# Attention with a routed expert layer: a slot's tokens as whole rows through DRAM, in place of quarter rows gathered straight

## The chip, the cores and the metric

The kernel runs on one core of a Trainium2 chip. The metric is the device time of one execution in microseconds (us). Before the change it is 1119.16 us, the median of 3 runs between 1118.36 and 1120.58. The core has a matmul engine (TensorE, PE in the rows), three engines for elementwise work (VectorE or DVE, ScalarE or ACT, GpSimd or POOL), a queue engine that does nothing but start transfers (SyncE or SP), an on-chip memory of 128 partitions and 16 DMA engines that all queues share.

## The reference

```
q, k, v: (8, 12, 448, 64)                       # batch, heads, positions, head size
attn = softmax(rmsnorm(q, g_q) @ rmsnorm(k, g_k).T / 8) @ v
x = attn as 3584 rows of 768                    # one row for each token, the 12 heads side by side
logits = x @ w_gate + modality_bias[modality_id]
e = argmax(logits);  p = softmax(logits)[e]     # one of 8 experts for each token
out[token] = p * (relu(x[token] @ w1[e]) @ w2[e])     # w1: 768 x 1024, w2: 1024 x 768
```

All is float32. The kernel splits an operand into a rounded high part and the rest, and makes a product out of three matmuls.

## The kernel before

**Attention.** The 96 heads are worked off as 48 units of two heads, each in 7 steps, so that step `n` belongs to unit `n // 7`. Every engine runs its instructions in the order in which the program issues them; one loop over `n` (from L1278) issues for each step what a table (`PLAN`) has due: the score matmuls `st` (L953), the matmuls with the values `av` (L992), the row sums `sums` (L1009, tiles `sm`), whose addends GpSimd forms in `csum` (L968, tiles `r2w`, `at_hhw`, `at_w2hb`), the transposes. SyncE starts the loads of q, k and v, small moves between partitions (L868), the row maxima of a unit (`mt`, L940, the move at L948) and the stores of finished rows of x to the DRAM tensor `x_d` (L1072). The second matmul of each `st` step reads the row that L948 moves, so that unit 47 can't begin its scores before its move has landed.

**Routing.** After each batch the logits give the expert of each token; `route_put` (L1152) scatters (token, weight) pairs of 8 bytes into lists in DRAM, `l_d`, four scatters a batch. GpSimd issues them, and each waits until the one before has landed. Those of batches 6 and 7 are issued in slots 0 and 1.

**Experts.** The tokens of an expert are cut into blocks of 256, called slots; 14 of them (`NSTAT`) are always run, with the same program. A slot is 144 matmuls of the first product (`mm1_half`, tiles `ph`) and 96 of the second (`mm2_step`, tiles `py`). In the loop over slots (L1444) 8 half blocks of the first product and 16 steps `b_` of the second are issued in turn, and other work is hung between them at `beat` numbers: the half blocks are beats 0 to 7, step `b_` is beat `b_ + 8`. The work of one slot for later ones is: weight loads (`wload`, GpSimd), the splits `split1` and `split2` (ACT and VectorE, tiles `w1w`, `w2ha`, `w2lw`), the second half `hlw` of the hidden values (VectorE), the results' scatter to `out` (GpSimd, from the tile `yw`), and the tokens.

**A slot's tokens.** The list is fetched from `l_d` (`get`, L337, tile `ltn`), eight entries to a partition, and the same in each of four groups of 32 partitions. `fin` (L348) makes from it the indices of quarter rows (`xi`) and an ordered copy (`ltq`). `xload` (L495) issues 8 gathers on GpSimd, each with one quarter row of 768 bytes for each of 128 partitions: group g of 32 partitions holds quarter g of all 256 tokens. `xturn` (L513) then transposes on VectorE 32 by 32, in three parts, from `xrw` into a piece of `yw`; two copies (tiles `xw`) follow, and those are the operands of the first product. `yw` also holds the results on their way out, so a part of `xturn` waits for the scatter of the slot before it. `xrw` has two halves: slot s uses half s % 2. Slot 0 is gathered during unit 45 (L1374), slot 1 in the section after the attention loop (L1421), slot 2 in slot 0, slot 3 at the start of slot 2 (L1457), and every later slot two slots ahead at the steps `XLB` (L1501).

Of the kernel before, what the change touches and what calls it, by code (L numbers as in the profile page):

```python
# [9 lines left out]
F32 = mybir.dt.float32  # L10
# [56 lines left out]
def kernel(  # L67
# [24 lines left out]
    l_d = dp.tile([NE * NT, 2], F32, name="l_d")  # L92

# [53 lines left out]
    def gate_consts():  # L147
        GP.tensor_copy(out=m1, in_=modr.rearrange("p b (c w) -> p (b c) w", w=2)[:, :, 0])
        GP.tensor_scalar(out=m0, in0=m1, scalar1=-1.0, scalar2=1.0, op0=ALU.mult, op1=ALU.add)
        shp = [CP, B * NCH, NE]  # L150
        GP.tensor_tensor(out=ball, in0=m0.unsqueeze(2).to_broadcast(shp),
                        in1=bia[:, 0:1, :].to_broadcast(shp), op=ALU.mult)
        GP.tensor_tensor(out=btmp, in0=m1.unsqueeze(2).to_broadcast(shp),
                        in1=bia[:, 1:2, :].to_broadcast(shp), op=ALU.mult)
        GP.tensor_tensor(out=ball, in0=ball, in1=btmp, op=ALU.add)
        for tf, ti in iotas:
            GP.tensor_copy(out=tf, in_=ti)
        for g in range(1, 4):
            GP.memset(i_q[32 * g : 32 * g + 32], float(g))
        V.scalar_tensor_tensor(out=i_j, in0=i_q, scalar=-32.0, in1=i_pt[:, 0:1], op0=ALU.mult, op1=ALU.add)  # L160
        V.scalar_tensor_tensor(out=i_pn[:, 0:1], in0=i_j, scalar=8.0, in1=i_q, op0=ALU.mult, op1=ALU.add)
        V.tensor_scalar(out=i_pn[:, 1:2], in0=i_pn[:, 0:1], scalar1=4.0, scalar2=None, op0=ALU.add)
        V.tensor_copy(out=i_qi, in_=i_q.to_broadcast([128, 8]))
        GP.tensor_scalar(out=ie8, in0=i_e[:, 0:NE], scalar1=float(NE), scalar2=None, op0=ALU.add)
        GP.tensor_scalar(out=i_ebase, in0=i_e[:, 0:NE], scalar1=float(NT), scalar2=None, op0=ALU.mult)
# [21 lines left out]
    ltn = cp.tile([128, NSTAT, 8, 2], F32, name="ltn")  # L187
    lto = cp.tile([128, NS1 + NS2 - NSTAT, 2, 2], F32, name="lto")
    ltq = cp.tile([128, NSTAT, 2, 2], F32, name="ltq")
    xi = cp.tile([128, NSTAT, 8], I32, name="xi")  # L190
    i_q = cp.tile([128, 1], F32, name="i_q")
    V.memset(i_q, 0.0)
    i_j = cp.tile([128, 1], F32, name="i_j")
    i_pn = cp.tile([128, 2], F32, name="i_pn")
    i_qi = cp.tile([128, 8], I32, name="i_qi")

    def entry(s, t):
        return ltq[:, s, t] if s < NSTAT else lto[:, s - NSTAT, t]
# [24 lines left out]
    def tables(nm, ns, cnt, nb, taken, e_prev, half_blocks=None):  # L223
# [69 lines left out]
        V.tensor_scalar(out=eb[:, 0:nn], in0=js[:, 0:nn], scalar1=float(NE * NT - TB), scalar2=0.125,  # L293
                        op0=ALU.min, op1=ALU.mult)
        V.tensor_scalar(out=lr, in0=eb[:, 0:nn], scalar1=i_j[:, 0:1], scalar2=None, op0=ALU.add)
        ix = tl("ix", s2)
        for a, b_, pt in ((0, nn, i_pn), (nn, ns, i_pt)):
            if a < b_:
                sp = [128, b_ - a, 2]
                V.tensor_tensor(out=ix[:, a:b_], in0=js[:, a:b_].unsqueeze(2).to_broadcast(sp),  # L300
                                in1=pt.unsqueeze(1).to_broadcast(sp), op=ALU.add)
# [28 lines left out]
    def lists(nm, s0, ns, tb):  # L330
# [4 lines left out]
        rows = l_d.rearrange("(r w) c -> r (w c)", w=8)  # L335
# [12 lines left out]
        def fin(a, n):  # L348
            r, d = slice(a, a + n), slice(s0 + a, s0 + a + n)
            if s0 + a < NSTAT:  # L350
                V.scalar_tensor_tensor(out=xi[:, d], in0=ltn[:, d, :, 0].bitcast(I32), scalar=4.0,
                                       in1=i_qi.unsqueeze(1).to_broadcast([128, n, 8]),
                                       op0=ALU.mult, op1=ALU.add)
                for g in range(4):
                    p = slice(32 * g, 32 * g + 32)
                    V.tensor_copy(out=ltq[p, d], in_=ltn[p, d].rearrange("p s (t w) c -> p s t w c", t=2)[:, :, :, g])
                tid = ltq[:, d, :, 0].bitcast(I32)
            else:
                o = slice(s0 + a - NSTAT, s0 + a + n - NSTAT)
                tid = lto[:, o, :, 0].bitcast(I32)  # L360
# [131 lines left out]
    def xv(s):  # L492
        return view(xrw, 2 * DM * (s % 2), 128, 8, DM // 4)

    def xload(s, gs_=range(8)):  # L495
        tb, i = tb_of(s)
        if s < NSTAT:
            x = xv(s)
            src = x_d[:NT1] if s < NS1 else x_d[:]
            for g in gs_:  # L500
                G.indirect_dma_start(out=x[:, g], out_offset=None,
                                     in_=src.rearrange("t (g d) -> (t g) d", g=4),
                                     in_offset=IOFF(ap=xi[:, s, g : g + 1], axis=0))
            return x
# [246 lines left out]
    if True:  # L751
# [487 lines left out]
        XLB = (1, 2, 3, 5, 6, 7, 9, 10)  # L1239
# [38 lines left out]
        for n in range(P["start"], NJ * NU):  # L1278
# [95 lines left out]
            if n == NJ * (NU - 3) + 4:  # L1374
                xload(0)
# [45 lines left out]
        xload(1)  # L1421
# [22 lines left out]
        for s in range(NSTAT):  # L1444

            beat = {}
            if s + 1 < NSTAT:
                for g, (m, c) in enumerate(zip(XTB, XCB) if s else zip(XTB0, XCB0)):
                    at(beat, m, lambda m=m, c=c, g=g: at(beat, c, xturn(s + 1, g)))
            if s > 0:  # L1450
# [5 lines left out]
                if s == 2:  # L1456
                    at(beat, 1, lambda: xload(3))  # L1457
# [23 lines left out]
            for b_ in range(16):  # L1481
# [19 lines left out]
                if s != 1 and s + 2 < NSTAT and b_ in XLB:  # L1501
                    xload(s + 2, (XLB.index(b_),))
# [68 lines left out]
```

## Time and profile before

| | |
|---|---|
| median of 3 runs | 1119.16 us (1118.36 to 1120.58) |
| the profiled execution | 1117.16 us, of which its span is 1115.4 us |
| PE busy | 1056.9 us (95%) |
| VectorE, ScalarE, GpSimd busy | 791.8, 697.7 and 765.0 us |
| mean granted TensorE clock | 0.972 of full speed |
| gathers of quarter rows | 112 on GpSimd, 148.1 us busy, mean 1323 ns |
| DMA by SyncE, by GpSimd | 88.58 MB, 41.89 MB |

All times in rows are counted from the start of the span. The clock has two levels, 2.4 GHz (1.00 in the rows) and 1.2 GHz (0.50); a number between them is a mean over a stretch. A row that names L52 or L53 was recorded through a helper (`Deferred`, L47), and its tiles tell what it is. In the table of stages the attention ends at about 595 us, slot 0 runs to 631, slot 1 to 681, and slot 2 to 719.

### The profile page before, as it was taken

To read this page: it belongs to the slowest core of one execution; us is meant where nothing else is said; L and a number is where in the kernel's file an instruction comes from. 1 tells how busy PE (TensorE), PEld (TensorE's weight loads), DVE (VectorE), ACT (ScalarE), POOL (GpSimd) and SP (SyncE) were. 2 spreads that over 40 slices of the span, in tenths; PEclk is the share of its full clock that TensorE was granted. 3 is DMA by queue.
4 is the path that set the end of the run, shared out by engine and by line. 5 is a ranking of instruction groups with operands and counts; after the bars stand their busy time and mean duration, and the time that the engine had idled before them with its cause. 6 is when DMAs were issued, how large, how long until landed. Compare 5 with 4: busy or idle time off the path is not lost.

```text
span 1115.4 us, 19222 instructions
## 1 busy us (share of the span) xinstructions
PE 1056.9 (95%) x6536; PEld 812.6 (73%) x6536; DVE 791.8 (71%) x1402; ACT 697.7 (63%) x1293; POOL 765.0 (69%) x775
## 2 busy tenths in 40 slices
PE   8799999999999999998989959999999999999994
PEld 7444555555555555554547949999999999999994
DVE  5575788998789988889668947677556676556640
ACT  6686888878787788875644624446445555455520
POOL 6777777778777798777876747888555674565451
PEclk8899999999999999999989979999999999999998
DMA  8675667667677777664735221111163111111250
GB/s 187 149 170 122 157 171 182 147 153 174 145 183 154 174 156 164 165 141 101 213 84 177 29 43 45 44 44 57 50 234 101 44 57 31 44 58 57 85 200 32
DMA packets 133051, 131.80 MB, mean 118 GB/s; under 512 B 71192, under 2 KB 126924, under 8 KB 132176
## 3 DMA queue, kind: packets, MB, share of 16 engines
q1 hardware_dynamic: 110212, 88.58, 33.9%
q0 software_dynamic: 22704, 41.89, 12.3%
q8 instruction: 54, 0.88, 0.4%
q14 instruction: 53, 0.43, 0.1%
q10 hardware_dynamic: 28, 0.01, 0.0%
HBM read 139.39 MB, written 22.38 MB: 145 GB/s over the span
## 4 chain that ended last, share of the span: by engine, by line
PE 70%; DVE 7%; DMA 7%; POOL 6%; issue 6%; ACT 2%; SPq 1%; POOLq 0%; DVEq 0%; ACTq 0%
PE ph L547 17%; PE py L577 16%; PE av L999 12%; PE st L960 12%; PE sa L932 4%; PE tr L855 3%; DMA w1w<-xw 2%; DVE at_hlw L52 2%; POOL xrw L52 2%; PE xt L1056 2%; PE sm L1014 2%; POOL r2w L52 1%; DMA l_d<-lt,posi 1%; DVE xw L52 1%; DMA xrw<-x_d,xi 1%
## 5 line engine op out<-in xcount | busy, mean ns | idle before, releaser
L547 PE MATMUL ph<-xw,w1w 128*128 128x256 f32 x2016 | 245.8, 283 | 1.0 <-ACT xw L52 0.6
L547 PEld LDWEIGHTS ph<-xw,w1w 128*128 128x128 f32 x2016 | 243.8, 192 | 2.8 <-issue 1.4
L52 DVE TENSOR_REDUCE at_hlw<-sa 128x1 f32<-128x448 f32 x336 | 205.9, 617 | 44.5 <-PE sa L932 24.7
L960 PE MATMUL st<-w1w 128*128 128x448 f32 (+1 forms) x480 | 176.8, 418 | 0.0
L52 POOL DMA_INDIRECT xrw<-x_d,xi x112 | 148.1, 1323 | 36.0 <-issue 32.0
L52 ACT ACTIVATE r2w<-st 128x448 f32<-128x448 f32 x168 | 91.0, 544 | 62.0 <-PE st L960 54.7
L932 PE MATMUL sa<-w1w 128*128 128x448 f32 (+1 forms) x288 | 111.4, 388 | 16.3 <-DVE at_hlw L52 9.2
L52 POOL TENSOR_TENSOR r2w<-r2w 128x448 f32<-128x448 f32 (+1 forms) x72 | 82.1, 1140 | 58.6 <-DVE r2w L52 20.1
L960 PEld LDWEIGHTS st<-w1w 128*128 128x128 f32 (+1 forms) x480 | 85.4, 192 | 46.0 <-ACT r2w L52 17.1
L577 PE MATMUL py<-w2lw,hhw 128*128 128x384 f32 x448 | 115.3, 338 | 2.8 <-DVE w2lw L52 2.8
L52 DVE TENSOR_TENSOR w1w<-r,w1w 128x768 fp32r<-128x768 f32 x112 | 106.4, 979 | 8.0 <-ACT w1w L52 7.0
L52 ACT ACTIVATE hhw<-ph 128x512 fp32r<-128x512 f32 x56 | 33.5, 597 | 122.1 <-PE ph L547 122.1
L52 ACT CAST w1w<-xw 64x448 fp32r<-64x448 f32 x188 | 105.5, 561 | 3.4 <-issue 1.4
L52 ACT ACTIVATE at_w2lw<-st 128x448 f32<-128x448 f32 x168 | 90.6, 544 | 23.8 <-PE st L960 19.0
L52 DVE TENSOR_TENSOR w2lw<-r2w,w2ha 128x1536 fp32r<-128x1536 f32 x28 | 49.1, 1757 | 78.3 <-ACT w2ha L52 76.3
L960 PE MATMUL st<-w1w,w2ha 65*128 65x448 f32 x288 | 102.3, 375 | 1.8 <-DMA w1w<-xw 1.8
L52 POOL DMA_INDIRECT r2w<-in_moe_w_dram,tb_vi x48 | 49.6, 1033 | 77.8 <-DVE w2lw L52 71.4
L52 ACT CAST w1w<-r 128x768 fp32r<-128x768 f32 x112 | 95.2, 901 | 5.4 <-DMA r<-in_moe_w_dram,ta_wi 5.4
L52 POOL TENSOR_TENSOR xrw<-r,at_hlw 112x512 f32<-112x512 f32 x95 | 98.0, 1051 | 0.5
L577 PEld LDWEIGHTS py<-w2lw,hhw 128*128 128x128 f32 x448 | 82.0, 190 | 3.4 <-DVE w2lw L52 3.4
L52 ACT ACTIVATE yw<-py,ltq 128x384 f32<-128x384 f32 x55 | 29.3, 579 | 83.0 <-PE py L577 81.4
L52 POOL TENSOR_TENSOR r2w<-r2w,at_w2lw 64x448 f32<-64x448 f32 (+1 forms) x48 | 55.3, 1151 | 34.8 <-DVE r2w L52 15.6
(320 smaller groups left out, 2244.6 us busy)
## 6 DMA issues: line engine op xcount, KB each, us to landing
w1w<-xw SPq DMA_DIRECT2D x312, 112.0 KB
r<-in_q_dram SPq DMA_DIRECT2D x48, 224.0 KB
r<-in_k_dram SPq DMA_DIRECT2D x48, 224.0 KB
w2ha<-xw SPq DMA_DIRECT2D x72, 112.0 KB
x_d<-at_w2hb SPq DMA_DIRECT2D x8, 672.0 KB
x_d<-yw SPq DMA_DIRECT2D x8, 672.0 KB
r2w<-in_v_dram SPq DMA_DIRECT2D x48, 96.0 KB
at_w2lw<-in_v_dram SPq DMA_DIRECT2D x48, 96.0 KB
```

The lines of the kernel that those rows point to most:

```text
L52: return fn(*a, **kw)
L547: PE.matmul(ps[:, i], lhsT=lt_, rhs=rt_[:, c], start=n == 0, stop=n == 17)
L577: PE.matmul(ps[n][:, :384], lhsT=lt_[:, j, 128 * t : 128 * t + 128], rhs=rt_[:, 384 * n : 384 * n + 384], start=j == 0 and m == 0, stop=j ...
L855: PE.transpose(sp[:, c], src[:, c], idn[:CP, :CP])
L932: PE.matmul(ps[:, :S], lhsT=t["qq"][r, h, a : a + 128], rhs=t["kk"][h][r], start=True, stop=True)
L960: PE.matmul(ps[:, :S], lhsT=l, rhs=t["qq"][:, h] if first else t["ql"][:, h], start=first and (j != 3 or h == 0), stop=not first and (j != ...
L999: PE.matmul(t["av"][64 * h : 64 * h + 64, :S], lhsT=vv[r, u % 3, j], rhs=t["p"][r, j], start=c == 0, stop=c == 3)
L1014: PE.matmul(R[g][32 * i : 32 * i + 32, :S], lhsT=sel[:, m], rhs=T[u + i // 2]["cs"][:, i % 2], start=m == 0, stop=False, tile_position=(0, ...
L1056: PE.transpose(ps[:CP, 128 * c : 128 * c + 128], T[u]["xt"][:, c * CP : (c + 1) * CP], idn)
```

## The change

The list is now fetched with two entries to a partition, so that partition p holds tokens 2p and 2p + 1. A slot's tokens are gathered with two operations (`xgather`), each of 128 whole rows of 3072 bytes. `xfetch` then has SyncE store the two as 256 rows into a DRAM tensor of the slot (`xg_d[s]`, 768 KB), and load them from there in four transfers, each of one quarter of all rows into 32 partitions. `xturn` reads the same layout as before. The loaded form has now one place for all slots, the first half of `xrw`; the gathered rows lie in that place for slots 0 and 1 and in the second half for the others. The index arithmetic (`xi`, `ltq`, `i_j`, `i_pn`, `i_q`, `i_qi`) is gone. The gathers of slot 0 are issued at two steps of unit 45, and the fetch at the last; those of slot 3 at the end of slot 1 instead of the start of slot 2, and the three transposes of slot 3 come three beats later, as those of slot 1 do. From slot 4 on a slot has gathers at steps 2 and 5 of the second product and the fetch at step 7.

```
+    xg_d = [dp.tile([TB, DM], F32, name=f"xg{s}") for s in range(NSTAT)]
...
-                V.scalar_tensor_tensor(out=xi[:, d], in0=ltn[:, d, :, 0].bitcast(I32), scalar=4.0,
-                                       in1=i_qi.unsqueeze(1).to_broadcast([128, n, 8]),
-                                       op0=ALU.mult, op1=ALU.add)
-                for g in range(4):
-                    p = slice(32 * g, 32 * g + 32)
-                    V.tensor_copy(out=ltq[p, d], in_=ltn[p, d].rearrange("p s (t w) c -> p s t w c", t=2)[:, :, :, g])
-                tid = ltq[:, d, :, 0].bitcast(I32)
+                tid = ltn[:, d, :, 0].bitcast(I32)
...
     def xv(s):
-        return view(xrw, 2 * DM * (s % 2), 128, 8, DM // 4)
-
-    def xload(s, gs_=range(8)):
-        tb, i = tb_of(s)
-        if s < NSTAT:
-            x = xv(s)
-            src = x_d[:NT1] if s < NS1 else x_d[:]
-            for g in gs_:
-                G.indirect_dma_start(out=x[:, g], out_offset=None,
-                                     in_=src.rearrange("t (g d) -> (t g) d", g=4),
-                                     in_offset=IOFF(ap=xi[:, s, g : g + 1], axis=0))
-            return x
+        return view(xrw, 0, 128, 8, DM // 4)
+
+    def xs_(s):
+        return view(xrw, 0 if s < 2 else 2 * DM, 128, 2, DM)
+
+    def xgather(s, t):
+        src = x_d[:NT1] if s < NS1 else x_d[:]
+        G.indirect_dma_start(out=xs_(s)[:, t], out_offset=None, in_=src,
+                             in_offset=IOFF(ap=entry(s, t)[:, 0:1].bitcast(I32), axis=0))
+
+    def xfetch(s):
+        SY.dma_start(xg_d[s].rearrange("(t p) d -> p t d", t=2), xs_(s))
+        for g in range(4):
+            SY.dma_start(xv(s)[32 * g : 32 * g + 32],
+                         xg_d[s][:, DM // 4 * g : DM // 4 * (g + 1)].rearrange("(b p) d -> p b d", p=32))
...
-        XLB = (1, 2, 3, 5, 6, 7, 9, 10)
+        XLB, XFB = (2, 5), 7
...
-            if n == NJ * (NU - 3) + 4:
-                xload(0)
+            for t in range(2):
+                if n == NJ * (NU - 3) + 4 + t:
+                    xgather(0, t)
+            if n == NJ * (NU - 3) + 6:
+                xfetch(0)
...
-        xload(1)
+        xgather(1, 0)
+        xgather(1, 1)
+        xfetch(1)
...
-                for g, (m, c) in enumerate(zip(XTB, XCB) if s else zip(XTB0, XCB0)):
+                for g, (m, c) in enumerate(zip(XTB, XCB) if s not in (0, 2) else zip(XTB0, XCB0)):
...
-                if s == 2:
-                    at(beat, 1, lambda: xload(3))
...
-                if s != 1 and s + 2 < NSTAT and b_ in XLB:
-                    xload(s + 2, (XLB.index(b_),))
+                if s + 2 < NSTAT:
+                    for t_, m in enumerate((15, 15) if s == 1 else XLB):
+                        if b_ == m:
+                            xgather(s + 2, t_)
+                    if b_ == (15 if s == 1 else XFB):
+                        xfetch(s + 2)
```

## Rows read from the trace of the kernel before

**Rows 1.** Busy time by stage: stretch, length, engines (instructions), TensorE clock, DMA share, GB/s.
```profile
...
555.00:575.00 20.00, 16.55 (x77) 7.87 (x77) 14.99 (x29) 8.31 (x16) 16.22 (x16) 0.92 0.43 125
...
645.00:665.00 20.00, 10.59 (x67) 9.76 (x65) 5.94 (x11) 3.66 (x5) 10.26 (x11) 0.81 0.27 57
665.00:685.00 20.00, 15.94 (x87) 15.95 (x88) 14.88 (x41) 9.51 (x13) 12.52 (x10) 0.77 0.09 22
...
703.00:720.00 17.00, 15.52 (x82) 14.89 (x81) 14.90 (x22) 8.80 (x14) 14.56 (x9) 0.90 0.09 22
720.00:1060.00 340.00, 340.00 (x2409) 340.00 (x2408) 223.45 (x271) 179.56 (x231) 210.68 (x175) 1.00 0.23 72
```

**Rows 2.** The same columns at the end of attention, by 2 us.
```profile
...
572.00:574.00 2.00, 1.35 (x2) 0.18 (x2) 0.83 (x2) 0.00 (x0) 1.92 (x3) 0.50 0.00 0
...
578.00:580.00 2.00, 2.00 (x8) 0.95 (x8) 0.69 (x1) 1.06 (x3) 1.92 (x2) 0.80 0.81 247
```

**Rows 3.** TensorE in order of time: start, us, instruction, idle before it and releaser.
```profile
...
572.65 1.70 PE L1014 MATMUL sm<-at_hhw,sel 128*32 128x448 f32 x2 [1.95 <-POOL at_hhw L52]
...
578.62 1.17 PE L960 MATMUL st<-w1w 128*128 128x448 f32 x4
...
669.06 1.01 PE L577 MATMUL py<-w2hb,hlw 128*128 128x384 f32 x2 [11.16 <-DVE hlw L52]
```

**Rows 4.** GpSimd in order of time.
```profile
...
558.46 0.97 POOL L52 DMA_INDIRECT xrw<-x_d,xi  x1 [0.80 <-PE sm L1021]
...
567.61 0.94 POOL L52 DMA_INDIRECT xrw<-x_d,xi  x1 [0.30 <-issue]
...
604.39 0.97 POOL L52 DMA_INDIRECT xrw<-x_d,xi  x1 [1.66 <-PE xt L1056]
...
616.29 1.56 POOL L52 DMA_INDIRECT xrw<-x_d,xi  x1 [0.30 <-issue]
...
660.14 0.96 POOL L52 DMA_INDIRECT l_d<-lt,posi  x1 [4.61 <-DMA l_d<-lt,posi]
...
686.86 2.48 POOL L52 DMA_INDIRECT out_dram<-yw,la_oi  x1 [0.30 <-issue]
```

**Rows 5.** The chain that ended last: start, us, what.
```profile
...
250.03 2.21 DMA w1w<-xw
...
625.24 7.71 DMA l_d<-lt,posi
...
647.04 5.41 DMA l_d<-lt,posi
...
661.40 5.13 DMA out_dram<-yw,la_oi
...
700.03 2.66 DMA xrw<-x_d,xi
```

**Rows 6.** VectorE in order of time.
```profile
...
615.28 3.43 DVE L52 TENSOR_TENSOR w2lw<-r2w,w2hb 128x1536 fp32r<-128x1536 f32 x2 [0.68 <-ACT w2hb L52]
...
620.95 2.15 DVE L52 STREAM_TRANSPOSE yw<-xrw 128x512 f32<-128x512 f32 x2
...
666.55 1.07 DVE L52 STREAM_TRANSPOSE yw<-xrw 128x512 f32<-128x512 f32 x1 [8.02 <-DMA out_dram<-yw,la_oi]
...
703.01 1.15 DVE L52 STREAM_TRANSPOSE yw<-xrw 128x512 f32<-128x512 f32 x1 [7.21 <-DMA xrw<-x_d,xi]
```

**Rows 7.** The queue of SyncE in order of time.
```profile
...
564.71 0.79 SPq L948 DMA_DIRECT2D w1w<-xw  x1
577.01 0.64 SPq L1072 DMA_DIRECT2D x_d<-yw  x1
```

**Rows 8.** DMA issues: median us from issue to landing.
```profile
...
xrw<-x_d,lto POOLq DMA_INDIRECT x2, 7.4
```

**Rows 9.** GpSimd in order of time, later slots.
```profile
...
805.40 0.97 POOL L52 DMA_INDIRECT xrw<-x_d,xi  x1 [0.30 <-issue]
```

**Rows 10.** VectorE in order of time, later slots.
```profile
...
834.97 1.14 DVE L52 STREAM_TRANSPOSE yw<-xrw 128x512 f32<-128x512 f32 x1
```

More of the change, by code (lines that the diff above doesn't have):

```diff
@@ L157, in gate_consts @@
             GP.tensor_copy(out=tf, in_=ti)
[L158 to L163, printed above, removed]
         GP.tensor_scalar(out=ie8, in0=i_e[:, 0:NE], scalar1=float(NE), scalar2=None, op0=ALU.add)
@@ L186 @@
     V.memset(run0, 0.0)
-    ltn = cp.tile([128, NSTAT, 8, 2], F32, name="ltn")
+    ltn = cp.tile([128, NSTAT, 2, 2], F32, name="ltn")
     lto = cp.tile([128, NS1 + NS2 - NSTAT, 2, 2], F32, name="lto")
[L189 to L195, printed above, removed]
     def entry(s, t):
-        return ltq[:, s, t] if s < NSTAT else lto[:, s - NSTAT, t]
+        return ltn[:, s, t] if s < NSTAT else lto[:, s - NSTAT, t]
     state = {"run": run0}
@@ L292, in tables @@
         lr = tl("lr", [128, nn], I32)
-        V.tensor_scalar(out=eb[:, 0:nn], in0=js[:, 0:nn], scalar1=float(NE * NT - TB), scalar2=0.125,
+        V.tensor_scalar(out=eb[:, 0:nn], in0=js[:, 0:nn], scalar1=float(NE * NT - TB), scalar2=0.5,
                         op0=ALU.min, op1=ALU.mult)
-        V.tensor_scalar(out=lr, in0=eb[:, 0:nn], scalar1=i_j[:, 0:1], scalar2=None, op0=ALU.add)
+        V.tensor_scalar(out=lr, in0=eb[:, 0:nn], scalar1=i_pt[:, 0:1], scalar2=None, op0=ALU.add)
         ix = tl("ix", s2)
-        for a, b_, pt in ((0, nn, i_pn), (nn, ns, i_pt)):
+        for a, b_, pt in ((0, nn, i_wt), (nn, ns, i_pt)):
             if a < b_:
@@ L334, in lists @@
             tb["o2"] = [cp.tile([128, no, 2], I32, name=f"{nm}_o{n}") for n in range(2)]
-        rows = l_d.rearrange("(r w) c -> r (w c)", w=8)
+        rows = l_d.rearrange("(r w) c -> r (w c)", w=2)
         def get(a, n):
@@ L492, in xv, with xload @@
     def xv(s):
-        return view(xrw, 2 * DM * (s % 2), 128, 8, DM // 4)
-    def xload(s, gs_=range(8)):
-        tb, i = tb_of(s)
-        if s < NSTAT:
-            x = xv(s)
-            src = x_d[:NT1] if s < NS1 else x_d[:]
-            for g in gs_:
-                G.indirect_dma_start(out=x[:, g], out_offset=None,
-                                     in_=src.rearrange("t (g d) -> (t g) d", g=4),
-                                     in_offset=IOFF(ap=xi[:, s, g : g + 1], axis=0))
-            return x
+        return view(xrw, 0, 128, 8, DM // 4)
[10 more added lines that the diff above has]
+                         xg_d[s][:, DM // 4 * g : DM // 4 * (g + 1)].rearrange("(b p) d -> p b d", p=32))
+    def xload(s):
         xr = []
```

## The prediction

> **What bounds the kernel now.** I read the table of stages first. From 720 to 1060 us TensorE is busy 340.00 of 340.00 us at full clock [rows 1]: there nothing that the change takes from GpSimd or VectorE can count, and only a token that comes too late could. What can be won lies before 720, where three stages show TensorE idle or slow: 555 to 575 (16.55 of 20 us, clock 0.92), 645 to 685 (10.59 and 15.94 of 20, clock 0.81 and 0.77) and 703 to 720 (15.52 of 17, clock 0.90) [rows 1]. The timelines of the engines then tell who is waited for. At the end of attention TensorE waits for a row sum that GpSimd forms; GpSimd is late because the 8 gathers of slot 0 stand before it, from 558.46 to 568.55 [rows 3, 4]. The idle time there is 20 - 16.55 = 3.45 us, and afterwards the clock is granted at 0.50 until about 578.7, which costs some 3 us more [rows 1, 2]. In slot 1 TensorE stands 11.16 us until 669.06 for `hlw`, which VectorE could not form because it was itself held until 666.55 by a transpose into `yw`; that waits for a results' scatter that GpSimd issued only at 661.40 [rows 3, 5, 6]. The scatter stands behind the sixth of the list scatters (660.14), each of which waits for the landing of the one before [rows 4, 5]. In slot 2 VectorE waits 7.21 us, until 703.01, for the gathers of slot 3 [rows 6]. So the bound is TensorE with three holes, and GpSimd's queue is behind each of them.
>
> **The change part by part.** The sum is made on the profiled execution, 1117.16 us with a span of 1115.4; the 1.76 us around the span I leave. The median of the runs is 2.0 us above it, and I carry that over at the end.
>
> *Prices of transfers.* A quarter-row gather of 96 KB takes 2.66 us from issue to landing [rows 5], and a 672 KB store of x ran at 247 GB/s [rows 2, 7]. I take 2.3 us plus the bytes at 247 GB/s for each: a whole-row gather (384 KB) 3.9 us, the store (768 KB) 5.5, the four loads together (768 KB) 5.5. From both sides: 2.66 for a gather (as if the bytes were free), and 7.4, the only whole-row gathers before, which ran beside weight loads [rows 8]. An issue on SyncE is 0.64 us [rows 7].
>
> *End of attention, slot 0.* Six of 8 gathers leave GpSimd, about 7.5 us at the spacing of 1.25 to 1.5 us [rows 4], and the first sum of unit 45 goes between the remaining two. The sums are then done at about 564, before TensorE asks for them at 568.3 (572.65 less 3.45 idle and 0.9 of work between), and hole one goes: 6.5 us. Next in line is unit 47's score step, which stood at 578.62 [rows 3]; the 5.97 us from 572.65 to it, at half clock, are 3.0 at full, so it could now start near 571. But `xfetch(0)` is put on SyncE's queue ahead of four loads of v and of the move of unit 47's row maxima, which was issued at 564.71 [rows 7] and without which those scores can't end. The second gather is issued at about 560.4 and landed at 564.3; only then can the store start, landed at 569.8; then the four loads are issued until 572.4, the four v loads until 574.9, the move at 574.9, landed 2.2 us later [rows 5], 577.1. So TensorE stands about 6 us again, at a point that it reached at 578.9 before, and pays the low clock again, about 2.5 us as 572 to 578.7 did [rows 2]. The lead of 1.8 us is spent: I put this part at 0. Bounds: 5.5 us won if the move is not held up, and 4 lost if the gather takes 7.4. The tokens themselves land at about 575.5, and VectorE, which wanted them near 573, waits inside that same hole.
>
> *Slot 1.* Its gathers end at about 605.5 instead of 617.85 [rows 4]. The next thing in GpSimd's queue that has to wait is the second weight load, for the splits that end on VectorE at 618.71 [rows 6]; the first list scatter follows at about 620.1 instead of 625.24 [rows 5]: 5.1 us. From there to the sixth it was 34.9 us for five intervals. In some of these GpSimd was still busy with quarter-row gathers when the landing came; at a landing of 5.41 [rows 5] and 0.8 to the next issue they are five times 6.2, or 31. The sixth stands at 651.1, the results' scatter 1.26 later, landed 5.13 later [rows 5]: 657.5, and VectorE is free 9.0 us earlier than 666.55. TensorE's stop ends 9 us earlier, since the same work follows. Bounds: 4 (the start alone, less one slow issue) and 13.5 (no stop left). The tokens of slot 1 land near 619.5 (store behind x's last one), when VectorE wanted them at 620.95 [rows 6]; those of slot 2 near 646, when it gets there.
>
> *Slot 2.* The gathers of slot 3 now go ahead of the scatter that stood at 686.86 [rows 4], at 677.9 after the 9 us; landed 683.1, stored 688.6, loaded 694.4. Their transposes are three beats later and come behind `hlw`, where VectorE gets at about 692. It may wait 2 us, and then has 12 us to the next slot; in slot 0 the same work took from 620.95 to 630.4. The hole of 703 to 720 goes: 17 - 15.52 = 1.5 us and 10% of clock on the rest, 1.6: 3.1 us. Bounds 0 and 3.1.
>
> *Later slots.* The chain from the second gather to the last load is 3.9 + 5.5 + 5.8 = 15.2 us. The first gather of such a slot was at 805.40 and its first transpose at 834.97 [rows 9, 10]; the second gather is one place later, 806.7, so 28.3 us are there for 15.2. The transfers double in the stretch where DMA has a share of 0.23 [rows 1]. The index arithmetic of `fin` and the small constants at the start lie beside a busy TensorE: 0. Without that cover it would still be nothing, since VectorE has a third of its time free there, 223.45 of 340 us busy [rows 1].
>
> Sum: 0 - 9.0 - 3.1 = -12.1; 1117.16 - 12.1 = 1105.1, and 2.0 for the median gives **1107 us**.
>
> *A rule against the change.* The four loads write 32 partitions each; no transfer of such a shape stands in the rows, and the 247 GB/s are of one over 112 partitions. The Trainium skill, page "SBUF — State Buffer", section "Door 1: The DMA port swizzle (why `[64,N]` ≈ `[32,N]`)", says that 32 neighbouring partitions reach half of the 16 ports, and that two transfers to different halves don't make up for it. By that rule, loads at half the rate are the first rival.
>
> **The rivals.** *A, the loads go at half rate.* 768 KB at 123 GB/s are 6.4 us instead of 3.2; the move of unit 47 lies in the same queue behind them and lands near 580 instead of 577.1, so that the end of attention loses 3 us: 1110. For it: a form not seen; against it: four such loads are in flight together. Slots 3 to 13 still have 10 us left.
>
> *B, the list scatters set slot 1 by themselves.* If the interval between two of them stays at 34.9 / 5 = 7.0 us, because SyncE's new transfers run beside them, only the start moves, and 4 us come back instead of 9: 1112. For it: the sixth waited 4.61 us for a landing with nothing else to do [rows 4].
>
> *C, slower.* The chain of three transfers is longer than the 28.3 us of a slot. It decides from there on, in each of some 10 slots: at 31 us TensorE stops 2.7 us in each and pays about 2.5 for the clock, 52 us, so 1159. Against it: it would need twice the prices above.
>
> *D, the move is not held up.* The gathers land at 2.66 us and the store is quick, the row maxima arrive before TensorE: 5.5 us more, 1101.
>
> *E, nothing comes of it.* A new wait on VectorE (tokens of slot 2 or 3 late by 8 us) gives all back: 1118.
>
> **How the numbers follow.** Forecast 0.54, A 0.15, B 0.12, D 0.08, C 0.06, E 0.05. The range runs from D with slot 1 at its better bound, 1097, to near E, 1117; left out are C, E and a few hundredths below. About 0.2% (2.2 us) is what a measurement can tell from no change. Faster by more: the first four with 0.07 taken off for the forecast's own misses, 0.82. Same: E and 0.04 of these, 0.09. Slower: C and 0.03, 0.09.
>
> **What would show it.** In the changed kernel's trace: no wait of `sm` for `at_hhw` near 570, but one of `st` for the move of row maxima, which on SyncE's queue stands behind four loads near 575; the first list scatter at about 620 and the sixth at about 651; the stop for `hlw` in slot 1 of 2 to 7 us instead of 11.16; no stop in slot 2; and 720 to 1060 still without a hole, shifted. I am wrong if TensorE's stages after slot 3 show idle time, if the stop in slot 1 ends at the same distance from the first list scatter as before, or if the hole at the end of attention is longer than about 9 us.

## The result, and the profile after

The kernel after takes 1102.99 us, the median of 4 runs (1101.42 to 1105.66), the kernel before 1119.87 in the same comparison (1118.36 to 1121.58): a ratio of 0.9851, interval 0.9825 to 0.9877. In a second comparison, made beside the experiments (a_again below), it was 1104.37 against 1114.75, 0.991 (0.9877 to 0.9943). So the gain is 10 to 17 us, and the forecast of 12 lies inside. The profiled execution took 1102.07 us with a span of 1100.1, 15.3 less than that of before.

The stages first, with the columns of [rows 1], each at the place of its counterpart.

```profile
550.00:570.00 20.00, 16.22 (x87) 8.35 (x85) 14.10 (x27) 9.74 (x19) 12.88 (x11) 0.96 0.78 218
638.00:658.00 20.00, 12.99 (x75) 12.67 (x74) 11.09 (x25) 6.03 (x9) 8.16 (x8) 0.81 0.20 52
658.00:678.00 20.00, 20.00 (x138) 20.00 (x138) 14.43 (x32) 10.79 (x14) 15.09 (x13) 0.94 0.20 50
686.00:703.00 17.00, 17.00 (x105) 17.00 (x104) 12.18 (x16) 10.42 (x16) 7.17 (x5) 1.00 0.69 191
703.00:1043.00 340.00, 340.00 (x2410) 340.00 (x2409) 218.57 (x237) 179.37 (x231) 120.00 (x115) 1.00 0.38 112
```

The hole at the end of attention is as long as before (3.78 us idle for 3.45; from 570 to 574 us the clock is then 0.50), the one in slot 1 is shorter, the one in slot 2 is gone, and behind it TensorE is busy throughout, though DMA's share went from 0.23 to 0.38. The two stops of TensorE, with what releases them:

```profile
568.90 1.46 PE L947 MATMUL st<-w1w 65*128 65x448 f32 x3 [3.78 <-DMA w1w<-xw]
...
654.97 1.01 PE L564 MATMUL py<-w2hb,hlw 128*128 128x384 f32 x2 [7.01 <-DVE hlw L52]
```

The first is no longer `sm` waiting for GpSimd [rows 3] but `st` waiting for the move of row maxima, as forecast. The chain that ended last shows why, piece by piece (start, us, what):

```profile
554.23 3.95 DMA xrw<-x_d,ltn
...
558.33 3.38 DMA xg<-xrw
...
563.65 0.45 SPq L758
...
565.94 2.83 DMA w1w<-xw
...
568.90 1.46 PE st L947 x3
```

SyncE waits for the second gather, issues the store, waits until that has landed, issues four loads and four loads of v, and only then the move. The second stop is answered by GpSimd's list scatters and by VectorE, the counterparts of [rows 4, 6]:

```profile
614.18 0.97 POOL L52 DMA_INDIRECT l_d<-lt,posi  x1 [0.30 <-issue]
...
645.58 1.18 POOL L52 DMA_INDIRECT l_d<-lt,posi  x1 [3.93 <-DMA l_d<-lt,posi]
647.06 1.01 POOL L52 DMA_INDIRECT out_dram<-yw,la_oi  x1 [0.30 <-issue]
```

```profile
652.46 1.07 DVE L52 STREAM_TRANSPOSE yw<-xrw 128x512 f32<-128x512 f32 x1 [5.03 <-DMA out_dram<-yw,la_oi]
...
689.83 2.16 DVE L52 STREAM_TRANSPOSE yw<-xrw 128x512 f32<-128x512 f32 x2 [1.82 <-DMA xrw<-xg]
```

VectorE is released at 652.46, still by the results' scatter (647.06) behind the sixth list scatter (645.58). Slot 3's tokens make it wait 1.82 us (forecast: 2), and TensorE not at all.

**Where the time went, stage by stage.** Four marks cut the span: unit 3's move of row maxima on SyncE, unit 46's, the end of TensorE's stop for `hlw`, and the last results' scatter. All are starts of rows in timelines; the columns "first scatter" and "stop's end" are counted from unit 46's move, and "first to sixth" is the time between those two list scatters.

| trace | unit 3's move | first scatter | first to sixth | stop's end | stop to last scatter | from there to the span's end |
|---|---|---|---|---|---|---|
| before | 65.2 | 70.5 | 34.9 | 114.4 | 433.3 | 13.0 |
| b_again | 63.7 | 68.0 | 30.9 | 107.4 | 434.2 | 13.0 |
| b_const_late | 62.4 | 68.9 | 32.2 | 109.9 | 442.2 | 13.2 |
| b_slot3 | 65.3 | 67.5 | 31.1 | 107.2 | 429.7 | 12.9 |
| after | 62.1 | 65.4 | 31.4 | 106.2 | 430.0 | 15.2 |
| a_again | 61.3 | 65.3 | 30.6 | 104.8 | 428.6 | 15.0 |
| a_const_back | 65.5 | 65.3 | 31.2 | 105.3 | 430.0 | 14.9 |
| a_six1 | 60.4 | 66.5 | 29.8 | 105.5 | 429.5 | 15.7 |
| a_six2 | 61.6 | 64.1 | 31.1 | 104.1 | 429.5 | 15.4 |
| a_eight | 61.1 | 69.8 | 32.0 | 110.9 | 429.4 | 16.6 |
| a_fetch_late | 60.5 | 61.8 | 31.0 | 102.6 | 428.9 | 14.8 |

By this the first pair's 15.3 us are 3.1 up to unit 3, 2.8 more up to unit 46 (554.7 to 548.8 in all), 8.2 from there to the stop's end, 3.3 to the last scatter, less 2.1 at the end. The 8.2 and 3.3 look like the forecast's 9.0 and 3.1. The other traces of before say that the agreement is partly luck: from unit 46 to the stop's end it needed 107.4, 109.9 and 107.2 us in them, not 114.4. Taking means instead, the change is worth 3.5 up to unit 3 (ten traces without the wait of the next section, these and a_turn2, a_best and a_best2, lie between 60.4 and 62.4; four with it between 63.7 and 65.5), 109.7 - 105.4 = 4.3 to the stop's end, 433.8 - 429.5 = 4.3 to the last scatter, less 2.0 at the end: 10.1 us, near the 10.4 of the second comparison. (Not in these means: b_slot3's last stretch, which it changes, and b_const_late's 442.2, which holds 2.99 us of an idle TensorE between 750 and 800, at a clock of 0.93 there.) Between units 3 and 46 executions differ by up to 13 us whatever the kernel (a_turn2 loses 7.1 us on before there, a_best2 wins 5.7), and I count nothing there.

### The profile page after: what moved, and what is told of

Same layout as the page of the kernel before. It is cut to its first block, busy times and chain, and to the rows that moved or that the text cites. A ratio compares the mean times of both kernels' runs of the same rounds, so it can differ in the third digit from the quotient of the medians.

```text
span 1100.1 us, 19179 instructions
## 1 busy us (share of the span) xinstructions
PE 1049.9 (95%) x6536; PEld 810.4 (74%) x6536; DVE 784.9 (71%) x1347; ACT 697.2 (63%) x1293; POOL 639.7 (58%) x688
## 4 chain that ended last, share of the span: by engine, by line
PE 74%; DVE 8%; DMA 6%; issue 5%; POOL 3%; ACT 2%; SPq 1%; POOLq 0%; ACTq 0%; DVEq 0%
PE ph L534 19%; PE py L564 19%; PE av L986 11%; PE st L947 11%; PE sa L919 4%; DVE at_hlw L52 3%; PE tr L842 3%; PE xt L1043 2%; PE sm L1001 2%; DMA w1w<-xw 1%; DVE xw L52 1%; DMA l_d<-lt,posi 1%; DVE r2w L52 1%; PE sa L914 1%; PE mt L930 1%
## 5 line engine op out<-in xcount | busy, mean ns | idle before, releaser
L52 DVE TENSOR_TENSOR w1w<-r,w1w 128x768 fp32r<-128x768 f32 x112 | 104.0, 957 | 9.9 <-ACT w1w L52 8.8
L52 ACT CAST w1w<-xw 64x448 fp32r<-64x448 f32 x188 | 105.5, 561 | 3.4 <-issue 1.4
L52 POOL DMA_INDIRECT out_dram<-yw,lb_oi x22 | 22.5, 1023 | 117.1 <-ACT yw L52 114.5
L52 ACT ACTIVATE yw<-py,ltn 128x384 f32<-128x384 f32 x55 | 29.3, 578 | 81.6 <-PE py L564 78.8
L919 PEld LDWEIGHTS sa<-w1w 128*128 128x128 f32 (+1 forms) x288 | 55.1, 191 | 27.9 <-DVE at_hlw L52 12.5
```

What stands on the lines that cost most here:

```text
L52: return fn(*a, **kw)
L919: PE.matmul(ps[:, :S], lhsT=t["qq"][r, h, a : a + 128], rhs=t["kk"][h][r], start=True, stop=True)
```

## The experiments

Ratios are to the kernel before on the same chip, with 95% intervals.

### The constants at the start

In the first attention steps the traces show what the forecast had put at 0. Of before, VectorE and then TensorE:

```profile
44.68 0.16 DVE L52 SCALAR_TENSOR_TENSOR i_j<-i_q,i_pt 128x1 f32<-128x1 f32 x1 [3.81 <-POOL i_q L52]
```

```profile
45.88 0.47 PE L932 MATMUL sa<-w1w 128*128 128x448 f32 x1 [3.20 <-DVE at_hlw L52]
```

The small operation on `i_q` waits 3.81 us for GpSimd; a row maximum stands behind it on VectorE, and TensorE's next `sa` behind that. The change deleted `i_q`. Two runs: b_const_late moves the operations in the kernel before, a_const_back puts them back into the kernel after.

```
# b_const_late, in the kernel before
+                at(pre["V"], n + 12, lane_consts)     # the four V operations, moved
# a_const_back, in the kernel after
+        for g in range(1, 4):
+            GP.memset(i_q[32 * g : 32 * g + 32], float(g))
+        V.scalar_tensor_tensor(out=i_j, in0=i_q, ...)  # and three more
```

> The kernel before, with only the four VectorE operations that make lane constants (i_j, i_pn twice, i_qi) issued twelve steps later in the first attention stage; tokens are still fetched as in the kernel before. Theory (the gain of about 6 us inside attention is a wait of VectorE at 44.68 us for GpSimd's memsets of i_q, which the change removed together with the constants): that wait of 3.8 us and TensorE's wait of 3.2 us behind it at 45.88 go, and the half clock right after it, so the time falls by 3 to 6 us, to 1114 to 1117. Rival 1 (the attention gain comes from something else that the change does, or is a difference between executions): within 1 us of the kernel before, 1119.9. Rival 2 (the wait goes and is given back by the end of attention): the trace shows no wait at 45 us, and the row-max move before 555 us stands where it stood.

> The kernel after, with the three memsets of i_q on GpSimd and the four VectorE operations on them put back where the kernel before has them; their results are not used. Theory (the constants' wait is worth 3 to 6 us): slower than the kernel after by 3 to 6 us, 1106 to 1109, with VectorE's wait for GpSimd near 44 us back in the trace. Rival (attention's gain lies elsewhere): 1103, as the kernel after.

b_const_late: 1113.89 us, 0.9971 (0.9942 to 1.0001). a_const_back: 1106.48 us, 0.9904 (0.9871 to 0.9937). In a_const_back the wait is back, on VectorE and behind it on TensorE:

```profile
45.02 0.16 DVE L52 SCALAR_TENSOR_TENSOR i_j<-i_q,i_pt 128x1 f32<-128x1 f32 x1 [3.85 <-POOL i_q L52]
```

```profile
46.22 0.47 PE L931 MATMUL sa<-w1w 128*128 128x448 f32 x1 [3.23 <-DVE at_hlw L52]
```

In b_const_late it is not there, and unit 3's move stands at 62.4 (65.2 in before). The theory holds as to the place: without the wait every trace is ahead at unit 3, b_const_late by 2.8 us, the ten on the mean by 3.5. On the whole time b_const_late's ratio makes 3.2 us (the medians 2.4), and its interval just reaches no change; a_const_back cannot be told from a_again by its ratio. So the 3.5 us are shown as far as unit 3; that they last to the end of the program is not shown. Of 5.9 us that the first trace of after had won at unit 46 against that of before, a_again has 2.9 there, and b_again, the kernel before itself, has 7.2 (547.49 against 554.69): a lead at that place says little about the kernel.

### The end of attention

```
-            if n == NJ * (NU - 3) + 6:
+            if n == NJ * (NU - 2) + 2:
                 xfetch(0)
```

> The kernel after, with slot 0's gathers, store and loads issued some 6 us later, behind the last unit's row-max move on SyncE's queue. Theory (the move stands behind the store's wait on SyncE and TensorE's stop of 3.8 us at 568.9 and the half clock behind it come from that): the stop and most of the half clock go, 4 to 6 us faster than the kernel after, about 1098. Rival (slot 0's tokens then end the stop in its place: the chain of gather, store and loads takes 12 us and starts later): 1102 to 1105, with TensorE waiting near 575 us for a transpose of the tokens.

Only the store and the four loads move; the gathers stay where they are.

a_fetch_late: 1099.24 us, 0.9841 (0.9803 to 0.9879), beside 0.9904 and 0.9899 of the two other variants of the kernel after on that chip. SyncE's queue and TensorE:

```profile
556.35 0.80 SPq L935 DMA_DIRECT2D w1w<-xw  x1
557.33 0.38 SPq L486 DMA_DIRECT2D xg<-xrw  x1
561.15 1.80 SPq L488 DMA_DIRECT2D xrw<-xg  x4
```

```profile
569.63 0.68 PE L947 MATMUL st<-w1w 128*128 128x448 f32 x2 [1.53 <-ACT at_w2lw L52]
```

The move is issued before the store, and of the stop of 3.78 us a wait of 1.53 for ScalarE is left. From unit 46's move to slot 0's first product it takes 27.2 us, and 27.4 and 26.6 in a_best and a_best2, which have the same edit, where after, a_again and a_const_back take 31.2 to 31.4: 4 us, the lower end of what was expected. At the end of the next stop 2 to 4 of them are left (102.6 us instead of 104.8 to 106.2). The store is issued 1.5 us later than in the kernel after, counted from unit 46's move (11.0 against 9.5 us), and TensorE does not wait for the tokens. The theory holds. By the ratios the run is some 6 us ahead of the two other variants, more than the stages account for; the rest is not traced.

### Slot 1: gathers ahead of and between the list scatters

```
# a_six1: behind slot 1's two gathers;  a_six2: between the list scatters
+        for g in range(6):
+            G.indirect_dma_start(out=xdum[:, g], in_=x_d[:NT1].rearrange("t (g d) -> (t g) d", g=12), ...)
# a_eight: both, those behind slot 1's with out=view(xrw, 2 * DM, 128, 8, DM // 4)[:, g] and g=4
```

> The kernel after with six more row gathers issued by GpSimd right behind slot 1's two, so that GpSimd issues eight there as in the kernel before; each brings 256 bytes a row (not 768) into a buffer that nobody reads, so that the issues come back and few of the bytes. Theory (slot 1's gain comes from GpSimd's issues that stood ahead of the list scatters): the first list scatter comes 4 to 6 us later against the attention's last row-max move, TensorE's stop behind it grows from 7 to 10 us, and the time is 3 to 6 us above the kernel after. Rival (the gain there comes from bytes and transfers, not from issues): within 1 us of the kernel after.

> The same six gathers, put where the kernel before had slot 2's other six, between the list scatters of slot 0's second product. Theory (these issues stretch the list scatters' interval): the interval goes from 6.3 back to about 7.0 us, the sixth scatter comes 3 to 4 us later, and the time is 2 to 4 us above the kernel after. Rival (a list scatter waits for the one before it to land, and an issue of 1.2 us fits into that wait): interval 6.3 and the time of the kernel after within 1 us; the first list scatter alone, then, carries slot 1's gain.

> The kernel after with twelve more row gathers: six of 768 bytes a row behind slot 1's two, into the half of the buffer where the kernel before put slot 1, and six of 256 bytes a row between the list scatters; nobody reads them. So GpSimd issues eight gathers for either slot again. Theory (slot 1's gain is that of the gathers' number and bytes before and between the list scatters): the first list scatter comes 4 to 5 us later against attention's end, the sixth 6 to 8 us, and the time is 5 to 8 us above the kernel after. Rival (GpSimd had slack there, since it waited for w2's buffers between the issues): first scatter 1 to 2 us later, no more than 2 us above the kernel after.

> The kernel after, unchanged, beside the experiments, so that they have a time of it on their own chip and a second trace of it. All theories: 0.985 of the kernel before. What it tells apart: whether the 5.9 us by which the first trace of it is ahead at 555 us is the change's or partly one execution's. Theory: 3.1 us of it come from the constants and stand in every execution; the rest (1.6 at 97 us and what is gained and lost between 250 and 550) differs between executions by some us. Rival: it stands at 5.9 again.

> The kernel before, unchanged, for another trace of its stages. Theory: VectorE waits 3 to 4 us near 44 us for GpSimd's memsets again, and from the last row-max move but one to the end of TensorE's stop behind the list scatters it takes 110 to 114 us, where the kernel after takes 105 to 106. Rival (slot 1's gain is one slow execution's): 106 to 108.

Measured: a_again 1104.37 us, 0.991 (0.9877 to 0.9943); a_six1 1106.55, 0.9916 (0.9884 to 0.9947); a_six2 1105.32, 0.9898 (0.9864 to 0.9932); a_eight 1106.01, 0.9935 (0.9901 to 0.997); b_again, the kernel before itself, 1.0005 (0.9962 to 1.0048). GpSimd in a_six1, then in a_eight:

```profile
599.11 0.98 POOL L52 DMA_INDIRECT xrw<-x_d,ltn  x1 [0.30 <-issue]
...
604.15 4.15 POOL L52 DMA_INDIRECT xdum<-x_d,ltn  x1 [0.30 <-issue]
...
620.00 1.38 POOL L52 DMA_INDIRECT l_d<-lt,posi  x1 [0.30 <-issue]
```

```profile
621.61 0.98 POOL L52 DMA_INDIRECT l_d<-lt,posi  x1 [0.30 <-issue]
...
645.56 0.97 POOL L52 DMA_INDIRECT l_d<-lt,posi  x1 [1.66 <-DVE w2lw L52]
...
653.64 0.96 POOL L52 DMA_INDIRECT l_d<-lt,posi  x1 [5.79 <-DMA l_d<-lt,posi]
```

The table has the rest. Counted from unit 46's move, six gathers of 256 bytes a row ahead of the lists put the first scatter back by 1.1 us only, with 768 bytes a row (a_eight) by 4.4, to 69.8, and the stop ends at 110.9, in the range of before. But this count also holds the end of attention, which differs between executions: from unit 46's move to slot 0's first product the traces of before take 32.7, 30.0, 30.8 and 29.5 us, those of after, a_again and a_const_back 31.2 to 31.4, a_six1 29.9. So slot 0's first product is the better mark. Here it is in before, then in after:

```profile
587.37 1.67 PE L547 MATMUL ph<-xw,w1w 128*128 128x256 f32 x12
```

```profile
580.20 1.67 PE L534 MATMUL ph<-xw,w1w 128*128 128x256 f32 x12
```

Counted from it, the first list scatter comes after 37.9 to 38.1 us in all four traces of before, after 34.0 to 34.1 in after, a_again and a_const_back, and after 34.0 in a_six2, 36.6 in a_six1 and 38.4 in a_eight. The change wins some 4.0 us here in every trace, and the six issues, with a third of their old bytes, bring 2.6 of them back, about half of what a_six1's theory expected. GpSimd's rows in the kernel after say why it is no more:

```profile
602.86 2.28 POOL L52 DMA_INDIRECT r2w<-in_moe_w_dram,ta_vi  x1 [3.43 <-DVE w2lw L52]
...
610.14 2.26 POOL L52 DMA_INDIRECT r2w<-in_moe_w_dram,ta_vi  x1 [3.71 <-DVE w2lw L52]
```

With two gathers it waits twice for VectorE to free w2's buffers; with eight (before, a_six1) these waits are gone, and the issues themselves set the time. With the old bytes (a_eight) nothing is left of the 4.0 us, but how much of that is the bytes' stays open: TensorE stood for some 3 us near 610 in that execution, ahead of the splits that free w2's buffers. Gathers between the scatters (a_six2) leave first to sixth at 31.1: an issue fits into the wait for the landing, and that rival holds. From the first scatter to the stop's end before takes 43.8, 39.4, 41.0 and 39.7 us, after, a_again and a_const_back 40.8, 39.5 and 40.0: outside one trace nothing to speak of is won there. In time a_six1 and a_six2 cost nothing that can be measured, and a_eight has 0.9935 against 0.991, about 2.8 us with overlapping intervals. b_again met its rival: VectorE waits 3.37 us near 44 us again, but the stop ends at 107.4, and first to sixth is 30.9. The 34.9 on which the forecast's second half of slot 1 rested is one execution's.

### The stop behind the list scatters

```
# a_turn2
-        tt = ... view(yw, 512 * g, 128, 2, 8, 32)
+        tt = ... view(xrw, 2 * DM + 512 * g, 128, 2, 8, 32) if s == 2 else ...
# a_best: with that and a_fetch_late's edit; slot 3's list operation, gathers, store and loads at beat 5 of slot 2,
# its transposes from beat 17 on
+                    at(beat, 5, late3)          # fin2(0, 3), xgather(3, 0), xgather(3, 1), xfetch(3)
# a_best2: with a_turn2's and a_fetch_late's edits, and
-                    at(beat, 23, part(state["fin2"], 0, 3))       # slot 1
+                    at(beat, 4, part(state["fin2"], 0, 3))        # slot 2
```

> The kernel after, with the transposes of slot 2's tokens written into a half of the gather buffer that is free at that time, so that they do not wait until slot 0's results have been scattered out of the buffer they otherwise share. Theory (that one wait, VectorE's 5.0 us at 652.46, makes TensorE's stop of 7.0 us at 655 and the half clock of about 10 us behind it): the stop goes, 6 to 9 us faster than the kernel after, about 1095 to 1097, less up to 3 us if slot 3's gathers are then late. Rival (the six list scatters hold slot 2's tokens or slot 3's lists anyway, so another wait takes the place): 1101 to 1104.

> The kernel after with slot 0's fetch behind the last row-max move, slot 2's transposes into the free half of the gather buffer, and slot 3's list arithmetic, gathers, store and loads, with its transposes, moved some 10 us later, so that VectorE doesn't stand before slot 3's list while slot 2's first product waits. Theory (the stop of 7.0 us behind the list scatters was moved to slot 2's first product, 5.4 us of TensorE, because VectorE waited 8.7 us for slot 3's list): both stops go, 8 to 12 us faster than the kernel after, about 1091 to 1095. Rival (slot 3's tokens now come too late for its first product, a third place of the same chain): TensorE waits 3 to 8 us at slot 3's first product, and the gain is that of the late fetch alone, 2 to 4 us.

> The kernel after with slot 0's fetch behind the last row-max move, slot 2's transposes into the free half of the gather buffer, and the one VectorE operation that needs slot 3's list (the addresses of its results) moved from the end of slot 1's second product into slot 2's first; slot 3's gathers stay where they are. Theory (of the stop of 7.0 us behind the list scatters 5.3 us came back as a stop in slot 2's first product, because VectorE stood 8.7 us before that one operation): TensorE has no stop over 3 us between slot 0 and slot 4, and the time is 6 to 11 us below the kernel after. Rival (the list of slot 3 holds its tokens as well, and they come too late): a stop of 3 us or more before slot 3's first product, and 2 to 5 us below the kernel after, what the late fetch is worth.

a_turn2: 1104.73 us, 0.9899 (0.9863 to 0.9935), no better than the kernel after. Its TensorE and VectorE:

```profile
658.46 0.61 PE L565 MATMUL py<-w2hb,hlw 128*128 128x384 f32 x2 [1.71 <-DVE hlw L52]
...
682.41 10.25 PE L535 MATMUL ph<-xw,w1w 128*128 128x256 f32 x72 [5.35 <-DVE hlw L52]
```

```profile
651.74 1.13 DVE L52 STREAM_TRANSPOSE xrw<-xrw 128x512 f32<-128x512 f32 x1 [3.42 <-DMA xrw<-xg]
...
679.89 0.17 DVE L52 CUSTOM_DVE_ANT_0 lb_oi<-ltn,tb_iv 128x12 uint16<-128x12 uint16 x1 [8.68 <-DMA ltn<-l_d,tb_lr]
```

The stop of 7 us shrinks to 1.71, and 5.35 us stand in slot 2: VectorE arrives sooner at the operation that needs slot 3's list, waits 8.68 us (3.57 in the kernel after), and `hlw` is behind it. a_best moved that operation and all of slot 3's fetch; by its order slot 4's tokens were loaded over slot 3's before these were transposed, so its slot 3 computes with slot 4's rows and its VectorE waits for slot 4's loads, 23.4 us. Its 1117.14 us, 1.0019 (0.9995 to 1.0043), therefore tell nothing of the theory. a_best2 moves the one operation: 1097.7 us, 0.9853 (0.9804 to 0.9902). Its VectorE and TensorE:

```profile
667.10 0.17 DVE L52 CUSTOM_DVE_ANT_0 lb_oi<-ltn,tb_iv 128x12 uint16<-128x12 uint16 x1 [4.66 <-DMA ltn<-l_d,tb_lr]
...
687.19 2.04 DVE L52 STREAM_TRANSPOSE yw<-xrw 128x512 f32<-128x512 f32 x2 [15.32 <-DMA xrw<-xg]
```

```profile
689.01 0.58 PE L535 MATMUL ph<-xw,w1w 128*128 128x256 f32 x1 [5.14 <-ACT xw L52]
692.57 20.24 PE L535 MATMUL ph<-xw,w1w 128*128 128x256 f32 x143 [2.97 <-DVE xw L52]
```

No stop in slots 1 and 2 any more, and 8.1 us before slot 3: the rival. The time from the eighth list scatter to the first transpose of slot 3's tokens tells why: 654.3 to 689.8, 649.1 to 686.8, 663.8 to 700.0 and 645.8 to 687.2 in after, a_fetch_late, a_turn2 and a_best2, 35.5 to 41.4 us. Slot 3 can start no earlier than that; waits removed ahead of it appear again further on. Not all of this time is waiting for landings. GpSimd in a_best2:

```profile
648.60 6.67 POOL L52 DMA_INDIRECT r2w<-in_moe_w_dram,ta_vi  x1 [0.30 <-issue]
...
660.95 2.34 POOL L52 DMA_INDIRECT ltn<-l_d,tb_lr  x1 [0.30 <-issue]
...
668.74 1.64 POOL L52 DMA_INDIRECT xrw<-x_d,ltn  x1 [0.30 <-issue]
```

Four weight loads (`r2w`) and a results' scatter are issued ahead of the fetch of the list, and two more weight loads ahead of slot 3's first gather. Whether another order on GpSimd shortens the chain was not tried. From unit 46's move to the last results' scatter a_best2 takes 533.5 us and a_fetch_late 531.5, where after, a_again and a_const_back take 533.3 to 536.1. So a_best2 is no faster than a_fetch_late there, and the late fetch is the one cause that the stages show for both. Their medians lie 4 to 7 us below those of the kernel after, on different chips; what is beyond the stages is not traced.

### Slot 2

```
# b_slot3, in the kernel before
-                if s == 2:
-                    at(beat, 1, lambda: xload(3))
+                if s == 1 and b_ == 15:
+                    xload(3)
# and XTB0, XCB0 for the transposes in slot 2 (of slot 3's tokens)
```

> The kernel before, quarter rows gathered as there, with slot 3's eight gathers issued at the end of slot 1 in place of the start of slot 2, and its transposes three beats later: the two moves of the change in slot 2 alone. Theory (the hole of slot 2 is a matter of when gathers and transposes stand, not of whole rows): no stop of TensorE near 705 us, and 2 to 4 us below the kernel before. Rival (eight gathers can't be issued in the time that two take, so the hole stays or moves to the list arithmetic): the time of the kernel before within 1 us.

b_slot3: 1110.41 us, 0.9962 (0.9929 to 0.9996). First b_again's stage, then b_slot3's, in the columns of [rows 1]:

```profile
685.00:702.00 17.00, 15.49 (x79) 14.85 (x78) 13.74 (x21) 8.73 (x13) 13.43 (x12) 0.90 0.14 37
```

```profile
690.00:707.00 17.00, 17.00 (x102) 17.00 (x101) 13.40 (x22) 9.88 (x14) 14.26 (x10) 1.00 0.15 44
```

The hole goes without whole rows, and the time from the stop to the last scatter is that of the kernel after, 429.7. The gain of slot 2 is the order's, not the whole rows'. In the whole time its size is uncertain: b_slot3's ratio makes 4.2 us, its median 1.4.

## Why the prediction came out right, step by step

- *The constants at the start, "beside a busy TensorE: 0"*: wrong. I looked at how busy VectorE is on average and not at what its operations wait for. 3.5 us by the traces, up to unit 3.
- *End of attention, 0*: right in its mechanism. The hole changed its cause, and a_fetch_late shows that the move behind the store and the loads is that cause. It came sooner than I put it, above all since the store landed after 3.38 us and not 5.5: the move was issued 17.1 us behind unit 46's (565.94 - 548.80), where the forecast had 574.9 - 554.7 = 20.2. From unit 46's move to slot 0's first product before takes 30.7 us on the mean and after 31.3, so the 0 was 0.6 us from it.
- *Slot 1, -9.0*: the end fits the pair of traces (-8.2 together with the step above), the size does not stand. Its first half, the first list scatter 5.1 us sooner, is right in its mechanism (GpSimd waits for the splits) and is 4.0 in every trace, counted from slot 0's first product. The forecast put the scatter 1.4 us behind the splits (620.1 - 618.71); in the kernel after it is 2.6 (611.55 to 614.18), since two weight loads are issued between. (Two gathers from 604.39 on end at about 606.6, not 605.5; nothing hangs on it, as the wait behind them ends later.) Its second half, five intervals of 6.2 in place of 7.0 us, was read from the one trace in which they were 7.0; elsewhere before has 6.2 to 6.4 already. The forecast called itself wrong if the stop ended at the same distance from the first list scatter as before: in the pair it is 40.8 us for 43.8, in the other traces 39.5 and 40.0 for 39.4 to 41.0, so by those the sign is there. Only the start moved and some 4 us came back, as rival B has it, though not for its reason: the interval is as short in before as after. From unit 46's move to the stop's end the gain is 4.3 on the mean.
- *Slot 2, -3.1*: right, 3.3 in the pair and 4.3 on the mean. The forecast named the earlier gathers and the later transposes; b_slot3 shows that these two moves together do it with quarter rows as well.
- *Later slots, 0*: right, 340.00 of 340.00 us busy.
- *Prices*: the gather of whole rows in the chain above took 3.95 us (forecast 3.9; the median of all 28 is 4.5), the store 3.38 (5.5). The four loads of a later slot are seen in the kernel after by 1 us, the columns as above (store issued 759.76, loads from 763.21):

```profile
761.00:762.00 1.00, 1.00 (x8) 1.00 (x7) 1.00 (x2) 1.00 (x3) 0.00 (x0) 1.00 1.00 402
...
765.00:766.00 1.00, 1.00 (x8) 1.00 (x7) 0.00 (x0) 0.00 (x0) 0.76 (x1) 1.00 1.04 303
766.00:767.00 1.00, 1.00 (x8) 1.00 (x7) 0.00 (x0) 0.00 (x0) 0.00 (x0) 1.00 1.12 160
767.00:768.00 1.00, 1.00 (x8) 1.00 (x7) 0.00 (x0) 0.00 (x0) 0.00 (x0) 1.00 1.02 215
768.00:769.00 1.00, 1.00 (x7) 1.00 (x6) 0.00 (x0) 0.00 (x0) 0.00 (x0) 1.00 0.75 106
```

  The store reaches 402 GB/s. The loads take 5.8 us from issue to the last microsecond (forecast 5.5). A results' scatter issued at 762.06 runs beside their first part; what the six microseconds from 763 to 769 moved, 1.18 MB, is the loads' 0.79 and such a scatter's 0.39. In 766 to 768 they move 160 and 215 GB/s with the engines' share at 1.12 and 1.02. The rule of the Trainium skill, page "SBUF — State Buffer", section "Door 1: The DMA port swizzle (why `[64,N]` ≈ `[32,N]`)", that 32 partitions reach half of the ports, fits these rates; no run here loads the same bytes over all 128 partitions, so it is not tested. Rival A's 3 us did not come of it, because the loads' landing is not what the move waits for; it waits for their issue.
- *The end of the program*: not forecast. From the last scatter to the span's end it takes 12.9 to 13.2 us in the four traces of before and 14.7 to 15.2 in those of after without extra gathers; no row of an engine stands there. 2.0 us lost, cause open.

So what becomes of the hole at the end of attention and of that in slot 2 was right in its mechanism, slot 1 in its first half, and that the sum of 12.1 us fits is partly luck: 3.5 us at the start that I had not seen stand against some 5 us in slot 1 that the change does not bring, beside 2.0 at the end. Of the 10.1 us in the table's means, 4.3 come from the two moves of slot 2 and 3.5 from the constants. The fetch of whole rows itself is left with the 4.3 us up to the end of slot 1's stop, and the 2.0 at the program's end, whose cause is open, come off the whole.

## What to carry to other kernels

A stage length from one trace carries that execution's scatter: where a term is a difference of intervals (7.0 against 6.2 us), it wants a second trace or a reason that holds without the number. Take the mark close to what is asked: counted from unit 46's move the first list scatter of before varies by 3 us between traces, counted from slot 0's first product by 0.2. An operation that is removed counts with what it waits for and with what stands behind it on its engine, however short it is itself. And where a serial chain (here eight scatters, each waiting for the one before) sets when the data of a later stage exist, removing waits ahead of that stage only moves the stop: shorten the chain.

## What the runs showed of the hardware that was not expected

The same kernel differs between executions far more than the first three runs suggested: before took 1103.93 to 1121.65 us on one chip (b_again's runs among them) and 1111.82 to 1127.0 on another. An indirect transfer's issue on GpSimd, mostly 0.95 to 1.0 us, took 4.15 us in a_six1's row above and 6.67 in a_best2's. The long ones go with VectorE. In the kernel before:

```profile
608.19 4.05 POOL L52 DMA_INDIRECT xrw<-x_d,xi  x1 [0.30 <-issue]
```

```profile
608.00 3.42 DVE L52 TENSOR_TENSOR w2lw<-r2w,w2ha 128x1536 fp32r<-128x1536 f32 x2
```

The issue ends 0.82 us behind VectorE's operations, which have two inputs. So it is in all 14 traces: each of the 46 issues of more than 3 us ends 0.75 to 0.90 us behind the end of such an operation. Some issues beside such operations are not long, and no run varies this alone, so that the one causes the other is not shown. And in a_eight TensorE stood 1.91 and 1.14 us near 610 us for nothing that the profile names, within a stretch of 12.19 busy us of 16 in which a_again has 16.00.
